# Three open PSUM tiles for the first items of a convolution and spectral-mixing kernel

## The chip, the core and the metric

The kernel runs on one core of a Trainium2 chip. Its time is the device time of one execution in microseconds (us); of several executions the median is given. The engines are TensorE (PE: matmuls; PEld: its weight loads), VectorE (DVE), ScalarE (ACT), GpSimd (POOL) and SyncE (SP). Each takes its own instructions in order, and they meet through semaphores.

## The reference

```python
x = causal_conv(x, softmax(weight))      # 7 taps, one set for each of 8 groups of 24 columns
X = rfft(x, axis=1)[:, :64]              # x: (8, 3264, 192)
Yr = Xr @ w_r[m] - Xi @ w_i[m]           # for each of 64 modes m: two 192 x 192 matrices
Yi = Xr @ w_i[m] + Xi @ w_r[m]
u = x + irfft(Y, n=3264)
out = u + relu(u @ w_ch)                 # (8, 3264, 192) float32
```

## The kernel before

Batches are taken in pairs: `q` (0 to 3) is a pair, and a row tile `t` has 128 rows (t = 0 to 24, and a half tile at the end). The order of the instructions on each engine is the order in which the program writes them; nothing is rescheduled.

Stage 1 loads x, convolves it on TensorE and accumulates the 64 modes. Stage 2 has three kinds of work in one loop over `g` = 0 to 15 (`mix(g)`, L452):

- **Mixing g** multiplies four modes with their two weight matrices: 12 matmuls (L457) into one of two PSUM banks, `low[0]` and `low[1]`. After every second one ScalarE copies the bank out (L466), TensorE transposes the halves into `low[2]` and `low[3]` (L473), and VectorE and ScalarE copy these to `yet` (L480, L482). The weights of g = 8 to 11 are loaded by GpSimd (L446) when mixing g - 8, which had the same buffer, has ended, those of 12 to 15 when mixing g - 4 has. For the last pair of mixings, 14 and 15, these steps are made one by one.
- **Transposes of x**: `c_bank` (L405) makes up to eight 128 x 128 transposes into one bank of a ring of four banks `r`; the helper `copy` brings the bank to `cc`, each third time by ScalarE (L378), else by VectorE (L380).
- **Products ahead**: the output takes `u @ w_ch`, of which the part `x @ w_ch` needs only `cc` and `wc`. For eight of the output's items, and for the half tiles (`c_halves`, L506), it is made in this loop (`c_ahead`, L521: 12 matmuls into two ring banks, two copies of 384 columns) and kept in SBUF. `FREED` (L597) says after which mixing.

`zw_lower(q)` (L561) multiplies the lower 32 modes of pair q with `w_ch` in a ring bank, and copies it to `zw` (L569, L571). It stands after mixings 8 to 11.

Stage 3 makes 53 items (`duos`). An item is two row tiles of a pair of batches, mostly the same t for two pairs: 128 x 768 values in a PSUM tile of two banks. Four such tiles (`za`, `zb`) are used in turn. `c_part(n)` (L531) puts the product with c into the tile with 12 matmuls; an item made ahead has it copied in by ScalarE instead (L717). Then follow `m_part(n, 0)` (L551, the inverse transform times w_ch), Relu in place (`relu`, L613), `m_part(n, 1)` on top (the inverse transform itself), the addition of x by VectorE (`finish`, L638) and the store: by SP for items 0 to 3, which are two neighbouring row tiles (L651, two stores each), by GpSimd for the others (L646). The upper 32 modes of pairs 2 and 3, `(2, 3)`, and the half tiles, `("h",)`, are entries of their own in the list, 25 and 44.

Between the stages stand, in this order: mixing 15, `c_part(0)`, the transposes of mixing 15, the first half of `c_part(1)`, the products of the upper modes of pairs 0 and 1 (L561) in `low[0]` and `low[2]`, their copies, and the second half of `c_part(1)`. Only the tiles of items 0 and 1 are open then; the other two take the place of `low`.

Of the kernel before, what the change touches and what calls it, by code (L numbers as in the profile page):

```python
# [19 lines left out]
def kernel(  # L20
# [32 lines left out]
    def sb(name, shape, dtype, **kw):  # L53
        return pool.tile([P] + shape, dtype, tag=name, name=name, **kw)
# [9 lines left out]
    cc = sb("cc", [NQ, CB, P], BF16, align_bytes=256)  # L64

    MH = MODES // 2
    ftab = sb("ftab", [NT + 1, 2 * MODES], BF16)
    ftab4 = ftab[:, :, :].rearrange("p t (h c m) -> p t h c m", h=2, c=2)

    fupper = sb("fupper", [NT, P], BF16)  # L70
    tabs = (ftab, fupper)

    HD = D // 2
    yet = sb("yet", [2, B, 2, MODES], BF16)


    mixa = sb("mixa", [3 * 2 * B * MODES], BF16)
# [8 lines left out]
    w1 = sb("w1", [3 * HD], BF16)  # L86
    wc = sb("wc", [3, D], BF16)
    ident = sb("ident", [P], BF16)
    perm = sb("perm", [P], BF16)
    ascale = sb("ascale", [1], F32)  # L90
    halfpi = sb("halfpi", [1], F32)
    xs = [sb(f"xs{i}", [2, D], BF16) for i in range(2)]
# [7 lines left out]
        return wts[g] if g < NW + NL else wts[(g - NW - NL) % NW]  # L100


    OB = 2 * 2 * 2 * D
    assert 6 * OB <= NW * WGB and OB == 12 * P

    def place(a):
        return a.bitcast(F32).rearrange("p (k d) -> p k d", k=2)
# [3 lines left out]

    slices = [place(arena[:, OB * i:OB * (i + 1)]) for i in range(6)]
    in_band = place(band[:, :, :].rearrange("p h c -> p (h c)")[:, 0:OB])
    in_cc = [place(cc[:, q, t:t + 12, :].rearrange("p k s -> p (k s)")) for t in (0, 12) for q in range(2)]

    ccf = cc[:, :, :, :].rearrange("p q (t j) s -> p q t (j s)", j=3).bitcast(F32)
# [33 lines left out]

    conv_stack, pp = psum_pool("pconv", "left")
    Z = [pp.tile([P, 2, 512], F32, tag=f"z{i}", name=f"z{i}") for i in range(2)]
    low_stack, pp = psum_pool("plow", "right")
    low = [pp.tile([P, 512], F32, tag=f"low{i}", name=f"low{i}") for i in range(4)]

    def slot(q, t):
        return NT * q + t
# [92 lines left out]
    def load_units(k0, k1):  # L250
        for k in range(k0, k1):
            load_unit(*units[k])
            if k in beside:
# [4 lines left out]
    nc.gpsimd.memset(ident[:], 0.0)  # L258
    nc.gpsimd.affine_select(out=ident[:], in_=ident[:], compare_op=ALU.not_equal, fill=1.0,
                            base=0, pattern=[[-1, P]], channel_multiplier=1)  # L260
    nc.gpsimd.memset(perm[:], 0.0)
    for h in range(2):
        for c in range(2):

# [94 lines left out]
    def xtrans(q, i, bank):  # L359
        tp = low[1 + bank][:, 0:3 * P].rearrange("p (j c) -> p j c", j=3)  # L360
        xsv = xs[q % 2][:, i, :].rearrange("k (p j) -> k j p", j=3)
        for j in range(3):
            nc.tensor.matmul(tp[0:64, j, :], xsv[:, j, :], ident[:], start=True, stop=True,  # L363
                             tile_position=(0, 0), skip_group_check=True)
            nc.tensor.matmul(tp[64:P, j, :], xsv[:, j, :], perm[:], start=True, stop=True,
                             tile_position=(0, 64), skip_group_check=True)
        b = 2 * q + i
        for h in range(2):
            nc.vector.tensor_copy(out=xt[:, h, :, b:2 * B:B, :],
                                  in_=tp[:, :, 64 * h:64 * h + 64].rearrange("p j (c m) -> p j c m", c=2))  # L370
# [78 lines left out]
    for g in range(NL + NW):  # L449
        load_w(g)  # L450

    def mix(g):  # L452
        yp = low[(g // 2) % 2][:, D * (g % 2):D * (g % 2) + D]
        for j in range(3):
            for p4 in range(4):
                m = 4 * g + p4
                nc.tensor.matmul(yp[32 * p4:32 * p4 + 2 * B, :], xt[:, m // MH, j, :, m % MH],  # L457
                                 wbuf(g)[:, p4, j, :], start=(j == 0), stop=(j == 2),
                                 tile_position=(0, 32 * p4), skip_group_check=True)
        if g < NW:  # L460
            load_w(g + NW + NL)
        elif g >= NW + NL:
            load_w(g + NW)

    def mix_copy(d, gs=slice(0, 2)):
        nc.scalar.copy(out=ymix[d % 2][:, gs, :],  # L466
                       in_=low[d % 2][:, 0:2 * D].rearrange("p (g d) -> p g d", g=2)[:, gs, :])

    def mix_trans(d, gs=slice(0, 2)):
        ets = [low[2 + t][:, :].bitcast(BF16)[:, 0:2 * P].rearrange("p (g k) -> p g k", g=2) for t in range(2)]  # L470
        for t in range(2):
            for g in range(gs.start, gs.stop):
                nc.tensor.transpose(ets[t][0:HD, g, :], ymix[d % 2][:, g, HD - HD * t:D - HD * t], ident[:])  # L473
        m = slice(8 * d + 4 * gs.start, 8 * d + 4 * gs.stop)
        for t in range(2):
            dst = yet[0:HD, t, :, :, m].rearrange("p b c m -> p c b m")
            srcv = ets[t][0:HD, gs, :].rearrange("p g (q k) -> p (g q) k", q=4)[:, :, 0:16].rearrange(
                "p m (c b) -> p c b m", c=2)
            if t == 0:
                nc.vector.tensor_copy(out=dst, in_=srcv)  # L480
            else:
                nc.scalar.copy(out=dst, in_=srcv)  # L482
# [71 lines left out]
    def zw_part(q, h, z):  # L554


        for t, w in enumerate((wm, w1)):
            for i in range(2):
                for c in range(2):
                    p0 = 64 * i + 32 * c  # L560
                    nc.tensor.matmul(z[p0:p0 + MH, HD - HD * t:2 * D - HD * t],  # L561
                                     yet[0:HD, t, 2 * q + i, c, MH * h:MH * h + MH], w[0:HD, :],
                                     start=(t == 0), stop=(t == 1), tile_position=(0, p0), skip_group_check=True)

    def zw_copy(q, h, z, act, w=slice(0, 4)):
# [7 lines left out]
    def zw_lower(q):  # L573
        next_bank()
        z = ring[(tbank[0] - 1) % len(ring)]
        zw_part(q, 0, z)
        zw_copy(q, 0, z, q % 2)

    duos = [((q, t), (q, t + 1)) for q in range(2) for t in (0, 2)]
    duos += [((q, t), (q + 1, t)) for q in (0, 2) for t in range(0 if q else 4, NF)]  # L580

    duos[-1:] = [(u,) for u in duos[-1]]
    for k, item in ((25, (2, 3)), (44, ("h",))):
        duos.insert(k, item)

    def is_zw(n):
# [2 lines left out]


    AHEAD = {}
    for (n1, n2), p1 in zip(((8, 13), (18, 23), (30, 35), (40, 48)), [in_band] + slices):
        (q, t1), (_, t2) = duos[n1][0], duos[n2][0]
        AHEAD[n1], AHEAD[n2] = four(p1), ccf[:, q:q + 2, t1:t2 + 1:t2 - t1, :]
        assert duos[n1] == ((q, t1), (q + 1, t1)) and duos[n2] == ((q, t2), (q + 1, t2)) and (q or t1 > 7)

    FREED = {8: (8,), 9: (13,), 12: (18, 23), 13: (30, 40), 14: (35, 48)}  # L597

    free = [in_cc[0], slices[4], slices[5], in_cc[1], slices[3]]
    LATER = {7: (in_band,), 9: (in_cc[2], in_cc[3]), 17: (slices[0],), 29: (slices[1],), 39: (slices[2],)}  # L600
    buffers = []
    for n, duo in enumerate(duos):
        for p in LATER.get(n, ()):
# [11 lines left out]
    def finish(n):  # L615
# [16 lines left out]
        if len(duo) == 1:  # L632
            nc.vector.tensor_tensor(out=ov[:, 0:2, :], in0=zt[:, :, 0:D], in1=xall[:, s[0], :, :], op=ALU.add)
            dst = bass.AP(tensor=out.tensor, offset=out.offset + (2 * q0 * S + P * t0) * D,
                          ap=[[D, P], [S * D, 2], [1, D]])
            (nc.gpsimd if n < N - 1 else nc.sync).dma_start(out=dst, in_=ov[:, 0:2, :])
            return
        nc.vector.tensor_tensor(out=o[:, :, :].rearrange("p k (i d) -> p i k d", i=2),  # L638
                                in0=zt[:, :, 0:2 * D].rearrange("p i (k d) -> p i k d", k=2),
# [13 lines left out]
    N = len(duos)  # L653
    items = [[duo, None] for duo in duos]

    def assign(Z):
        for k, item in enumerate(items):
            if k % 4 in Z:
                item[1] = Z[k % 4]

    PLAN = (2, 2, 3, 2, 3, 2, 2, 2, 3, 3, 3, 3, 99, 99, 99)
    for g in range(NG - 1):
        mix(g)
        if g == NG - 2:
            mix_copy(g // 2, slice(0, 1))
        elif g % 2:
            mix_copy(g // 2)
        some(PLAN[g], NT * (NQ - 1) if g < NW + NL - 1 else NT * NQ)
        for n in FREED.get(g, ()):
            c_ahead(n)  # L670
        if g == NG - 3:
            c_halves()
        if g == NG - 2:
            mix_trans(g // 2, slice(0, 1))
        elif g % 2:
            mix_trans(g // 2)
        if NG // 2 <= g < NG // 2 + NQ:
            zw_lower(g - NG // 2)
    ring_stack.close()
    stack, pp = psum_pool("pz0", "left")  # L680
    ctx.push(stack)
    assign({k: pp.tile([P, 2, 512], F32, tag=f"za{k}", name=f"za{k}") for k in (0, 1)})
    mix(NG - 1)
    mix_copy(NG // 2 - 1, slice(1, 2))
    c_part(0)
    mix_trans(NG // 2 - 1, slice(1, 2))
    c_part(1, (0,))
    for q in range(2):
        zw_part(q, 1, low[2 * q])
    for w in QUARTERS:  # L690
        zw_copy(0, 1, low[0], w == QUARTERS[1], w)
    zw_copy(1, 1, low[2], False)
    c_part(1, (1,))
    low_stack.close()
    stack, pp = psum_pool("pz1", "right")
    ctx.push(stack)
    assign({k: pp.tile([P, 2, 512], F32, tag=f"zb{k}", name=f"zb{k}") for k in (2, 3)})

    def set_up(n):

# [11 lines left out]
    for n in range(N + 1):  # L712
# [5 lines left out]
        elif given(n + 2):  # L718
            nc.scalar.copy(out=items[n + 2][1][:, :, 0:2 * D].rearrange("p k (a d) -> p k a d", a=2),
                           in_=halves.rearrange("p (k a) d -> p k a d", k=2))  # L720

        soon = given(n + 1) or given(n + 2) or given(n + 3) and not given(n - 1)
        if n > 0 and not soon and not given(n):
            set_up(n + 1)
        if 0 < n and not is_zw(n - 1):
            m_part(n - 1, 1)
            finish(n - 1)
        if n > 0 and soon:
            set_up(n + 2 if given(n + 1) else n + 1)


# [28 lines left out]
```

## Time and profile before

Nine runs of the kernel before have a median of 176.71 us (176.59 to 177.59). The profiled execution took 177.59 us, of which its trace covers a span of 174.1 us; 3.5 us lie around it. All times below are us from the start of that span.

| | PE | PEld | DVE | ACT | POOL | DMA |
|---|---|---|---|---|---|---|
| busy in the span | 147.1 (84%) | 108.2 (62%) | 119.4 (69%) | 105.7 (61%) | 100.6 (58%) | mean 231 GB/s |

The mixings start at 74.42, the last of them at 107.14. The first output item is added at 111.62 and its stores are issued from 112.60; the last addition ends at 168.18, and the transfers end in the stretch from 170 to 172. The granted TensorE clock is 1.00 of full speed in every stretch from 30 to 160. In a row of the timeline the columns are start, length, engine, line, operation, output<-input, shape and count, then in brackets the idle time before it and what ended it. A row can stand for several merged instructions; a matmul's length contains its way through the array, so the starts of neighbouring rows say more of TensorE's pace than the lengths do. In a row of the chain the columns are start, length and what ran.

### The profile page before, as it was taken

To read this page: it belongs to the slowest core of one execution; us is meant where nothing else is said; L and a number is where in the kernel's file an instruction comes from. 1 tells how busy PE (TensorE), PEld (TensorE's weight loads), DVE (VectorE), ACT (ScalarE), POOL (GpSimd) and SP (SyncE) were. 2 spreads that over 40 slices of the span, in tenths; PEclk is the share of its full clock that TensorE was granted. 3 is DMA by queue.
4 is the path that set the end of the run, shared out by engine and by line. 5 is a ranking of instruction groups with operands and counts; after the bars stand their busy time and mean duration, and the time that the engine had idled before them with its cause. 6 is when DMAs were issued, how large, how long until landed. Compare 5 with 4: busy or idle time off the path is not lost.

```text
span 174.1 us, 6407 instructions
## 1 busy us (share of the span) xinstructions
PE 147.1 (84%) x2768; PEld 108.2 (62%) x2768; DVE 119.4 (69%) x181; ACT 105.7 (61%) x149; POOL 100.6 (58%) x157
## 2 busy tenths in 40 slices
PE   0056659999999999797999999999999999999930
PEld 0034426666666666576788876887778678875720
DVE  1878653684875677354678785498889879887860
ACT  8166662636444643535566765678888788787820
POOL 7999999867967544353224400006776657666560
PEclk9999997999999999999999999999999999999985
DMA  4999999999999999999999992089898998999994
GB/s 44 164 174 188 190 190 190 193 190 192 190 193 187 200 207 205 207 209 204 207 207 206 206 203 45 4 274 349 339 349 323 362 357 350 361 359 349 314 369 182
DMA packets 44331, 40.17 MB, mean 231 GB/s; under 512 B 28800, under 2 KB 40656, under 8 KB 44304
## 3 DMA queue, kind: packets, MB, share of 16 engines
q0 software_dynamic: 41136, 37.59, 108.8%
q1 hardware_dynamic: 3168, 2.19, 3.9%
q8 instruction: 21, 0.34, 0.8%
q14 instruction: 6, 0.05, 0.1%
HBM read 39.40 MB, written 20.05 MB: 342 GB/s over the span
## 4 chain that ended last, share of the span: by engine, by line
PE 46%; POOL 19%; issue 14%; DVE 7%; DMA 5%; ACT 5%; POOLq 1%; DVEq 0%; ACTq 0%
POOL out_dram L646 17%; PE z L324 13%; PE low L350 9%; DMA arena<-in_moe_w_i_dram 5%; PE r L405 5%; PE low L405 4%; PE low L457 3%; DVE arena L203 2%; PE r L394 2%; PE za L531 2%; PE za L551 2%; PE zb L551 1%; PE low L363 1%; DVE xall L344 1%; POOL xall L165 1%
## 5 line engine op out<-in xcount | busy, mean ns | idle before, releaser
L165 POOL DMA_DIRECT2D xall<-in_x_dram x48 | 38.4, 807 | 5.6 <-DMA xall<-in_x_dram 3.2
L324 PE MATMUL z<-xall,band 64*64 64x192 bf16 (+3 forms) x816 | 27.5, 264 | 16.3 <-ACT band L209 10.5
L344 DVE CAST xall<-z 128x768 bf16<-128x768 f32 (+1 forms) x24 | 24.5, 1021 | 14.7 <-PE z L324 13.5
L646 POOL DMA_DIRECT2D out_dram<-arena x23 | 17.3, 754 | 29.8 <-DVE arena L638 27.3
L342 ACT CAST xall<-z 128x768 bf16<-128x768 f32 (+1 forms) x24 | 20.4, 851 | 22.3 <-PE z L324 21.2
L324 PEld LDWEIGHTS <-band 64*64 64x64 bf16 x816 | 18.3, 110 | 24.9 <-ACT band L209 10.9
L531 PEld LDWEIGHTS <-cc 64*128 64x128 bf16 x504 | 22.7, 94 | 6.2 <-issue 2.8
L613 ACT ACTIVATE za<-za 128x768 f32<-128x768 f32 (+1 forms) x26 | 19.9, 781 | 5.7 <-PE za L551 5.1
L613 ACT ACTIVATE zb<-zb 128x768 f32<-128x768 f32 (+1 forms) x26 | 20.1, 781 | 5.0 <-PE zb L551 4.6
L350 PE MATMUL low<-xall,ftab 128*128 128x384 bf16 x100 | 21.7, 344 | 0.0
L405 PEld LDWEIGHTS <-xall 128*128 128x128 bf16 x300 | 18.7, 105 | 3.3 <-issue 0.3
L380 DVE COPY cc<-r 128x1024 bf16<-128x1024 bf16 (+2 forms) x23 | 14.0, 631 | 6.1 <-PE r L405 2.7
L551 PEld LDWEIGHTS <-ftab 64*128 64x128 bf16 x220 | 14.1, 94 | 5.7 <-issue 1.9
L551 PE MATMUL zb<-mixa,ftab 64*128 64x384 bf16 (+1 forms) x112 | 17.4, 309 | 0.0
L551 PE MATMUL zb<-mixa,fupper 64*128 64x384 bf16 (+1 forms) x112 | 17.4, 308 | 0.0
L551 PE MATMUL za<-mixa,ftab 64*128 64x384 bf16 (+1 forms) x108 | 16.7, 308 | 0.5 <-ACT za L613 0.4
L551 PE MATMUL za<-mixa,fupper 64*128 64x384 bf16 (+1 forms) x108 | 16.7, 308 | 0.0
L446 POOL DMA_DIRECT2D arena<-in_moe_w_r_dram x12 | 7.4, 616 | 15.7 <-PE low L457 10.8
L646 POOL DMA_DIRECT2D out_dram<-cc x17 | 12.8, 754 | 4.6 <-DVE cc L638 2.9
L638 DVE TENSOR_TENSOR arena<-za,xall 128x768 f32<-128x768 f32 x14 | 13.3, 955 | 2.3 <-PE za L551 1.4
L531 PE MATMUL zb<-wc,cc 64*128 64x192 bf16 x258 | 14.5, 243 | 0.0
L531 PE MATMUL za<-wc,cc 64*128 64x192 bf16 x246 | 14.0, 243 | 0.3 <-DVE cc L638 0.2
(126 smaller groups left out, 243.2 us busy)
## 6 DMA issues: line engine op xcount, KB each, us to landing
out_dram<-arena POOLq DMA_DIRECT2D x23, 384.0 KB, 4.7
out_dram<-cc POOLq DMA_DIRECT2D x17, 384.0 KB, 4.7
xall<-in_x_dram POOLq DMA_DIRECT2D x24, 192.0 KB, 7.1
xall<-in_x_dram POOLq DMA_DIRECT2D x16, 240.0 KB, 6.6
arena<-in_moe_w_r_dram POOLq DMA_DIRECT2D x12, 288.0 KB, 9.2
arena<-in_moe_w_i_dram POOLq DMA_DIRECT2D x12, 288.0 KB, 9.3
out_dram<-band POOLq DMA_DIRECT2D x5, 384.0 KB, 4.7
xall<-in_x_dram POOLq DMA_DIRECT2D x8, 144.0 KB, 6.7
```

The source lines that it names most:

```text
L165: nc.gpsimd.dma_start(out=xall[:, s0:s0 + nf, i, :], in_=src)
L324: mm = nc.tensor.matmul(ov[c], band[r, h, c.start + shift + 64 * (r is UP and c is LO): c.start + shift + 64 * (r is UP and c is LO) + 64] ...
L342: nc.scalar.copy(out=dst, in_=srcv)
L344: nc.vector.tensor_copy(out=dst, in_=srcv)
L350: nc.tensor.matmul(xp, ftab[:, t, :], xall[:, slot(q, t), :, :], start=(t == 0), stop=False, skip_group_check=True)
L380: nc.vector.tensor_copy(out=out, in_=in_)
L405: nc.tensor.transpose(tp[:, P * k:P * k + P], src, ident[:])
L531: nc.tensor.matmul(zt[:, i, D * k:D * k + D], cc[r, q, 3 * t + j, :], wc[r, j, :], start=(k == 0 and j == 0), stop=False, skip_group_check ...
L551: nc.tensor.matmul(zt[:, i, D * k:D * (k + w)], tabs[c][r, t, :], zw[r, c, q:q + w, QUARTERS[which], :], start=False, stop=end and k + w = ...
L613: nc.scalar.activation(out=zt[:, :, 0:w], in_=zt[:, :, 0:w], func=ACT.Relu)
L638: nc.vector.tensor_tensor(out=o[:, :, :].rearrange("p k (i d) -> p i k d", i=2), in0=zt[:, :, 0:2 * D].rearrange("p i (k d) -> p i k d", k=2),
L646: nc.gpsimd.dma_start(out=dst, in_=ov)
```

## The change

Item 0 becomes two single items, one row tile each (numbers 0 and 1); there are 54 entries now, and each later one has a number that is one higher. Three PSUM tiles for the items (`z0` to `z2`, six banks) are opened after mixing 14, and `c_part(0)`, `c_part(1)` and `c_part(2)` stand there, ahead of mixing 15. They hold what the items 0 and 1 held before. For this the ring and the banks `low[0]` and `low[1]` are closed at that point, so that mixings 14 and 15 write to `low[2]`, the bank that the transposes of all mixings use too. The products ahead of eight items are spread differently: after mixings 8, 9, 10 and 11 one each, after 12 and 13 two each, none after 14 (before: one after 8 and 9, two after 12, 13 and 14). To have room for the result of the third, `yet`'s lower half, the end of `ftab` and `perm` are put into one piece of SBUF, `early`, that is free once the four `zw_lower` have run; these stand two by two after mixings 8 and 9. The items made ahead are now every fifth; the entries `(2, 3)` and `("h",)` stand at 26 and 34. One more buffer for finished items is free from the start.

```diff
+    ND = NG // 2
+    def mix_bank(d):
+        return low[d % 2] if d < ND - 1 else low[2]
...
-        ets = [low[2 + t][:, :].bitcast(BF16)[:, 0:2 * P].rearrange("p (g k) -> p g k", g=2) for t in range(2)]
+        ets = [low[2 + t][:, c:c + P].bitcast(BF16).rearrange("p (g k) -> p g k", g=2)
+               for t, c in enumerate((2 * D if d == ND - 1 else 0, 0))]
...
+    duos[0:1] = [(u,) for u in duos[0]]
     duos[-1:] = [(u,) for u in duos[-1]]
-    for k, item in ((25, (2, 3)), (44, ("h",))):
+    for k, item in ((26, (2, 3)), (34, ("h",))):
...
-    for (n1, n2), p1 in zip(((8, 13), (18, 23), (30, 35), (40, 48)), [in_band] + slices):
+    for (n1, n2), p1 in zip(((9, 14), (19, 24), (29, 39), (44, 49)), [in_band, in_early] + slices):
...
-    FREED = {8: (8,), 9: (13,), 12: (18, 23), 13: (30, 40), 14: (35, 48)}
+    FREED = {8: (9,), 9: (14,), 10: (19,), 11: (24,), 12: (29, 39), 13: (44, 49)}
...
+        if g in (NG // 2, NG // 2 + 1):
+            for q in range(2):
+                zw_lower(2 * (g - NG // 2) + q)
         for n in FREED.get(g, ()):
             c_ahead(n)
         if g == NG - 3:
             c_halves()
         if g == NG - 2:
+            ring_stack.close()
+            low_stack.close()
+            for k in range(3):
+                open_z(k, "left")
+                c_part(k)
             mix_trans(g // 2, slice(0, 1))
         elif g % 2:
             mix_trans(g // 2)
-        if NG // 2 <= g < NG // 2 + NQ:
-            zw_lower(g - NG // 2)
...
     mix(NG - 1)
-    mix_copy(NG // 2 - 1, slice(1, 2))
-    c_part(0)
-    mix_trans(NG // 2 - 1, slice(1, 2))
-    c_part(1, (0,))
+    mix_copy(ND - 1, slice(1, 2))
+    mix_trans(ND - 1, slice(1, 2))
     for q in range(2):
-        zw_part(q, 1, low[2 * q])
+        zw_part(q, 1, low[2 + q])
...
-    c_part(1, (1,))
...
-            (nc.gpsimd if n < N - 1 else nc.sync).dma_start(out=dst, in_=ov[:, 0:2, :])
+            (nc.sync if n < 2 or n == N - 1 else nc.gpsimd).dma_start(out=dst, in_=ov[:, 0:2, :])
...
+        if n == 1:
+            continue
+        if n == 2:
+            m_part(0, 1)
+            finish(0)
```

`mix_bank(d)` is new: the bank of the pair d of mixings, of ND = 8. `open_z(k, side)`, new too, opens tile k of the four and gives it to every fourth entry from k on.

More of the change, by code (lines that the diff above doesn't have):

```diff
@@ L66 @@
     MH = MODES // 2
-    ftab = sb("ftab", [NT + 1, 2 * MODES], BF16)
+    OB = 2 * 2 * 2 * D
+    YH = 2 * B * 2 * MH
+    early = sb("early", [NT * P + OB], BF16)
+    ftab = early[:, 0:(NT + 1) * P].rearrange("p (t k) -> p t k", t=NT + 1)
+    in_early = early[:, NT * P:NT * P + OB]
+    perm = early[:, (NT + 1) * P + YH:(NT + 2) * P + YH]
+    assert (NT + 2) * P + YH <= NT * P + OB
     ftab4 = ftab[:, :, :].rearrange("p t (h c m) -> p t h c m", h=2, c=2)
@@ L73 @@
     HD = D // 2
-    yet = sb("yet", [2, B, 2, MODES], BF16)
+    yupper = sb("yupper", [2, B, 2, MH], BF16)
+    yet = (early[:, (NT + 1) * P:(NT + 1) * P + YH].rearrange("p (t b c m) -> p t b c m", t=2, b=B, c=2), yupper)
     mixa = sb("mixa", [3 * 2 * B * MODES], BF16)
@@ L88 @@
     ident = sb("ident", [P], BF16)
-    perm = sb("perm", [P], BF16)
     ascale = sb("ascale", [1], F32)
@@ L100, in wbuf @@
         return wts[g] if g < NW + NL else wts[(g - NW - NL) % NW]
-    OB = 2 * 2 * 2 * D
     assert 6 * OB <= NW * WGB and OB == 12 * P
@@ L113 @@
     in_band = place(band[:, :, :].rearrange("p h c -> p (h c)")[:, 0:OB])
+    in_early = place(in_early)
     in_cc = [place(cc[:, q, t:t + 12, :].rearrange("p k s -> p (k s)")) for t in (0, 12) for q in range(2)]
@@ L152 @@
     Z = [pp.tile([P, 2, 512], F32, tag=f"z{i}", name=f"z{i}") for i in range(2)]
+    last_stack, pp = psum_pool("plast", "right")
+    low = [pp.tile([P, 512], F32, tag=f"low{i}", name=f"low{i}") for i in (2, 3)]
     low_stack, pp = psum_pool("plow", "right")
-    low = [pp.tile([P, 512], F32, tag=f"low{i}", name=f"low{i}") for i in range(4)]
+    low[0:0] = [pp.tile([P, 512], F32, tag=f"low{i}", name=f"low{i}") for i in (0, 1)]
     def slot(q, t):
@@ L260 @@
                             base=0, pattern=[[-1, P]], channel_multiplier=1)
-    nc.gpsimd.memset(perm[:], 0.0)
+    nc.gpsimd.memset(perm, 0.0)
     for h in range(2):
@@ L364, in xtrans @@
                              tile_position=(0, 0), skip_group_check=True)
-            nc.tensor.matmul(tp[64:P, j, :], xsv[:, j, :], perm[:], start=True, stop=True,
+            nc.tensor.matmul(tp[64:P, j, :], xsv[:, j, :], perm, start=True, stop=True,
                              tile_position=(0, 64), skip_group_check=True)
@@ L450 @@
         load_w(g)
+    ND = NG // 2
+    def mix_bank(d):
+        return low[d % 2] if d < ND - 1 else low[2]
     def mix(g):
-        yp = low[(g // 2) % 2][:, D * (g % 2):D * (g % 2) + D]
+        yp = mix_bank(g // 2)[:, D * (g % 2):D * (g % 2) + D]
         for j in range(3):
@@ L466, in mix_copy @@
         nc.scalar.copy(out=ymix[d % 2][:, gs, :],
-                       in_=low[d % 2][:, 0:2 * D].rearrange("p (g d) -> p g d", g=2)[:, gs, :])
+                       in_=mix_bank(d)[:, 0:2 * D].rearrange("p (g d) -> p g d", g=2)[:, gs, :])
     def mix_trans(d, gs=slice(0, 2)):
-        ets = [low[2 + t][:, :].bitcast(BF16)[:, 0:2 * P].rearrange("p (g k) -> p g k", g=2) for t in range(2)]
+        ets = [low[2 + t][:, c:c + P].bitcast(BF16).rearrange("p (g k) -> p g k", g=2)
+               for t, c in enumerate((2 * D if d == ND - 1 else 0, 0))]
         for t in range(2):
@@ L473, in mix_trans @@
                 nc.tensor.transpose(ets[t][0:HD, g, :], ymix[d % 2][:, g, HD - HD * t:D - HD * t], ident[:])
-        m = slice(8 * d + 4 * gs.start, 8 * d + 4 * gs.stop)
+        h, m0 = divmod(8 * d, MH)
+        m = slice(m0 + 4 * gs.start, m0 + 4 * gs.stop)
         for t in range(2):
-            dst = yet[0:HD, t, :, :, m].rearrange("p b c m -> p c b m")
+            dst = yet[h][0:HD, t, :, :, m].rearrange("p b c m -> p c b m")
             srcv = ets[t][0:HD, gs, :].rearrange("p g (q k) -> p (g q) k", q=4)[:, :, 0:16].rearrange(
@@ L561, in zw_part @@
                     nc.tensor.matmul(z[p0:p0 + MH, HD - HD * t:2 * D - HD * t],
-                                     yet[0:HD, t, 2 * q + i, c, MH * h:MH * h + MH], w[0:HD, :],
+                                     yet[h][0:HD, t, 2 * q + i, c, :], w[0:HD, :],
                                      start=(t == 0), stop=(t == 1), tile_position=(0, p0), skip_group_check=True)
@@ L595 @@
         assert duos[n1] == ((q, t1), (q + 1, t1)) and duos[n2] == ((q, t2), (q + 1, t2)) and (q or t1 > 7)
-    FREED = {8: (8,), 9: (13,), 12: (18, 23), 13: (30, 40), 14: (35, 48)}
-    free = [in_cc[0], slices[4], slices[5], in_cc[1], slices[3]]
-    LATER = {7: (in_band,), 9: (in_cc[2], in_cc[3]), 17: (slices[0],), 29: (slices[1],), 39: (slices[2],)}
+    FREED = {8: (9,), 9: (14,), 10: (19,), 11: (24,), 12: (29, 39), 13: (44, 49)}
+    free = [in_cc[0], slices[4], slices[5], in_cc[1], slices[3], slices[2]]
+    LATER = {8: (in_band,), 10: (in_cc[2], in_cc[3]), 28: (slices[0],), 43: (slices[1],)}
     buffers = []
@@ L654, with open_z @@
     items = [[duo, None] for duo in duos]
[L656 to L659, printed above, removed]
+    def open_z(k, side):
+        stack, pp = psum_pool(f"pz{k}", side)
+        ctx.push(stack)
+        zt = pp.tile([P, 2, 512], F32, tag=f"z{k}", name=f"z{k}")
+        for item in items[k::4]:
+            item[1] = zt
     PLAN = (2, 2, 3, 2, 3, 2, 2, 2, 3, 3, 3, 3, 99, 99, 99)
@@ L676 @@
             mix_trans(g // 2)
-        if NG // 2 <= g < NG // 2 + NQ:
-            zw_lower(g - NG // 2)
[L679 to L682, printed above, removed]
     mix(NG - 1)
-    mix_copy(NG // 2 - 1, slice(1, 2))
-    c_part(0)
-    mix_trans(NG // 2 - 1, slice(1, 2))
-    c_part(1, (0,))
+    mix_copy(ND - 1, slice(1, 2))
+    mix_trans(ND - 1, slice(1, 2))
     for q in range(2):
-        zw_part(q, 1, low[2 * q])
+        zw_part(q, 1, low[2 + q])
     for w in QUARTERS:
-        zw_copy(0, 1, low[0], w == QUARTERS[1], w)
-    zw_copy(1, 1, low[2], False)
-    c_part(1, (1,))
[L694 to L697, printed above, removed]
+        zw_copy(0, 1, low[2], w == QUARTERS[1], w)
+    zw_copy(1, 1, low[3], False)
+    last_stack.close()
+    open_z(3, "right")
     def set_up(n):
@@ L720 @@
                            in_=halves.rearrange("p (k a) d -> p k a d", k=2))
+        if n == 1:
[3 more added lines that the diff above has]
+            finish(0)
         soon = given(n + 1) or given(n + 2) or given(n + 3) and not given(n - 1)
-        if n > 0 and not soon and not given(n):
+        if n > 1 and not soon and not given(n):
             set_up(n + 1)
@@ L727 @@
             finish(n - 1)
-        if n > 0 and soon:
+        if n > 1 and soon:
             set_up(n + 2 if given(n + 1) else n + 1)
```

## The prediction

> **What bounds the kernel now.** First the busy time by stretch (columns: stretch, its length, busy PE, PEld, DVE, ACT, POOL, clock, DMA share, which can pass 1, GB/s):
>
> ```profile
> 90.00:100.00 10.00, 10.00 (x207) 8.34 (x205) 8.03 (x16) 6.91 (x11) 4.12 (x7) 1.00 1.21 205
> 100.00:110.00 10.00, 9.52 (x206) 6.88 (x205) 7.16 (x16) 5.44 (x13) 0.00 (x0) 1.00 0.64 110
> ...
> 120.00:130.00 10.00, 10.00 (x164) 7.84 (x161) 8.72 (x10) 8.18 (x12) 6.80 (x10) 1.00 0.90 346
> ```
>
> Ahead of the last mixing TensorE and the weight loads are both full; in the output TensorE is full and the stores come close. Then the chain of work that ended last, at the seam:
>
> ```profile
> 97.26 0.60 POOL arena L446
> 97.86 9.23 DMA arena<-in_moe_w_i_dram
> 107.14 0.45 PE low L457 x12
> 107.59 0.60 PE za L531 x12
> 108.78 0.60 PE low L561 x16
> 110.17 0.80 ACT za L613
> ```
>
> Mixing 15 waits for its weights until 107.14. How long TensorE itself has nothing to do there is in the timeline:
>
> ```profile
> 90.31 0.68 PE L521 MATMUL r<-wc,cc 64*128 64x192 bf16 x12
> 90.41 1.01 ACT L378 COPY cc<-r 128x1024 bf16<-128x1024 bf16 x1 [0.88 <-PE r L405]
> ...
> 104.57 0.42 PE L473 MATMUL low<-ident,xs 128*96 128x128 bf16 x4
> ...
> 104.92 0.45 PE L457 MATMUL low<-arena,mixa 128*16 128x192 bf16 x12
> ...
> 105.30 1.25 PE L521 MATMUL r<-wc,cc 64*128 64x192 bf16 x24
> ...
> 105.49 0.28 DVE L480 COPY yet<-low 96x128 bf16<-96x128 bf16 x1
> ...
> 106.47 0.31 PE L473 MATMUL low<-ident,xs 128*96 128x128 bf16 x2
> ...
> 107.14 0.45 PE L457 MATMUL low<-arena,mixa 128*16 128x192 bf16 x12 [0.35 <-DMA arena<-in_moe_w_i_dram]
> ...
> 108.12 0.31 PE L473 MATMUL low<-ident,xs 128*96 128x128 bf16 x2
> ...
> 108.41 0.22 DVE L480 COPY yet<-low 96x64 bf16<-96x64 bf16 x1 [1.08 <-PE low L473]
> ...
> 108.71 0.31 PE L561 MATMUL low<-wm,yet 96*32 96x288 bf16 x4
> ```
>
> Only 0.36 us (106.78 to 107.14) is free ahead of mixing 15. From 88.47, the start of mixing 8, on each row starts where the one before ends, apart from ring waits of 0.1 to 0.3. After 109.58, the first inverse transform, the waits show POOL waiting for VectorE's additions, and these for TensorE or Relu, never for a transfer; full stores land in a median of 4.3 to 5.0 us from the first part of the output to the last. So TensorE sets the pace there too: 5.41 us between the additions of items 10 and 15.
>
> **The change, part by part.** *Ahead of mixing 15.* All eight products ahead stay there and the products of the first three items (24 matmuls) join them: what the two products at 105.30 take, 106.47 - 105.30 = 1.17. Nothing leaves but the wait of 0.36. In the old order those products stood after mixing 15, where they were free: the first tile's ran while ScalarE copied the mixing out (107.52 to 107.96), the second's beside the copies to yet and zw.
>
> *Ring waits.* Ring banks are taken in turn. After mixing 8 there are now two `zw_lower` and then the first product ahead, so it falls on the third and fourth banks; the fourth holds the transposes that ScalarE copies from 90.41 to 91.42, and its matmuls alternate between both. Before, it took the first two and started at 90.31. TensorE would be there at 90.30 + 2 x 0.25 = 90.80 and goes on at about 91.45: 0.6, less the 0.17 that the old order waited: 0.4. After mixing 9 the product follows three banks of transposes and two `zw_lower`; VectorE has two copies of 0.5, one of 0.56 and one of 0.69 in its queue and frees the second bank near 94.95, TensorE comes at 94.5: 0.45, less the 0.16 there now: 0.3. The others meet a ScalarE copy once each (29 and 39): 0.15. Bounds: 0 and 1.3 in all; I take 0.85.
>
> *Mixing 14 in low[2].* It must wait until VectorE has copied the transposes of mixing 13 out. Now that copy ends at 105.77, while mixing 14 starts at 104.92 in another bank. VectorE comes to it late because it has the copies of two products and of the half tiles ahead of it; one of the two half-tile copies falls to ScalarE in the new count. From 0.3 (the copy follows the transposes at once, as at 108.41: 0.29 + 0.28 + 0.08, less 0.36) to 0.9 (as late as now); I take 0.6. Behind it on TensorE stand the new products, so they don't fill it.
>
> *Mixing 15 in the same bank.* It writes columns 192 to 383, the transposes just ahead lie in 384 to 511. By addresses nothing is to wait for, and in the old order mixing 15 waits for its weights alone. The Trainium skill, "PSUM — Partial Sum Buffer", section "PSUM bank collisions raise a hardware error", says that two engines must be kept apart by bank and quadrant and not by address; and the order of the changed kernel's instructions has such a wait on VectorE's copy. By the row at 108.12, copy and restart take until 108.71, 0.59 from the start of the transposes instead of 0.31: 0.28. By addresses the sum would be 0.28 less; I take the rule.
>
> *Weight loads.* Mixing 11 moves back by some 1.6 (0.25 + 0.6 + 0.7), and so does the last load, 97.86 to about 99.5. The DMA share is 1.2 until 104, so it queues either way; even with its own 9.23 in full it lands at 108.7, ahead of the new mixing 15. Nothing.
>
> Sum: 1.17 + 0.85 + 0.6 + 0.28 - 0.36 = 2.54 later, mixing 15 at 109.7.
>
> *From mixing 15 to the transform.* The transposes no longer stand behind 12 matmuls: 107.52 + 0.12 + 0.32 + 0.07 = 108.03 instead of 108.12: -0.09. The `zw` copies stay.
>
> *The first items.* In the old order 109.58 to the first store at 112.60 is 3.0. Now item 0 has 4 matmuls (0.16), way through the array and signal 0.26, a Relu of half the size (0.47 by the row at 166.40), 4 matmuls 0.16, 0.25, an addition of 0.55 (167.16): 1.85, so 1.2 sooner. But the tiles hold what two tiles held; the products of the next items (L531) follow the transform as before. Adding 0.16, 0.33 and 0.49 in their new order, the second half of item 2 ends 2.9 after the transform starts, that of old item 1 3.0 after. TensorE gains 0.1 for all that follows, and the early store only 0.4 MB of early transfers, while the stores later wait for TensorE. Two half Relus for one cost ScalarE 0.47 x 2 - 0.80 = 0.14, two half additions VectorE 0.55 x 2 - 0.96 = 0.14; they lie in the gaps of engines busy 8.2 and 8.7 of 10, and cost 0.14 without these. SP issues 2 + 6 stores where it issued 8.
>
> *Same work elsewhere.* Nine entries are given, 43 others are full or half, before as after; every fifth instead of nearly so. The half tiles' four stores (SP, 2.68 us at 160.98) move to the middle, with nothing behind them on SP. The sixth buffer frees nobody: no addition waits for a transfer. Bounds together -0.3 and +0.3; I take 0.
>
> In all 2.54 - 0.09 - 0.1 = 2.35. The profiled execution has 177.59 = 174.1 + 3.5; it would take 179.9. The median lies 0.9 under it: 176.71 + 2.35 = 179.06, say 179.0.
>
> A rule speaks against this: the Trainium skill ("Trainium Kernel Development and Optimization", best practices) judges TensorE's headroom by weight-load time, not by busy matmuls. From 88.4 to 104.9 PEld is busy 13.3 of 16.5 us; the 3.2 left would swallow the 1.17. But those 3.2 are not gaps: the 24 matmuls at 105.30 start 49 ns apart, and nothing starts in between. With the rule, the sum is 1.2; with the starts, 2.35.
>
> **The rivals.** (1) *Evictions keep up.* VectorE is busy 8.0 and ScalarE 6.9 of 10 there, so other waits may vanish as new ones come; no ring wait and mixing 14 late by 0.3: 1.17 + 0.3 + 0.28 - 0.36 - 0.2 = 1.2, 177.9. (2) *Weights late.* The loads queue behind fewer others and land as slowly as the first ones to cc did (11.4 instead of 9.3), at 110.9 for an issue at 99.5: 1.2 more, 180.2. (3) *Faster: the stores bound the output.* Place: the 5 us from 107 to 112 without any transfer. If the DMA share of 0.90 is all that it can give, the end follows the first store, which comes 1.2 sooner after the transform. It decides as soon as mixing 15 slips by less than 1.2, that is, if the products fill gaps that I took for work: 176.71 - 1.2 = 175.5 with no slip. For it: the transfers' tail of 4 us after the last addition. Against: stretches of 2 us with 0.98 beside others of 0.79, and POOL waiting for additions. (4) *It does nothing*: slip and early store cancel: 176.7.
>
> **How the numbers follow.** Main case 0.60 (178.3 to 179.8), rival 1 0.20 (177.2 to 178.3), rival 2 0.08, rival 3 0.08, rival 4 0.04. The range 177.2 to 180.1 leaves out the last two and half of rival 2, with some of the edges. A measurement of this kernel tells about 0.2% (0.35 us) from no change. Faster 0.08, same 0.04, slower 0.88.
>
> **What would show it.** Right: mixing 15 released by VectorE's copy and not by its weights, near 109.7; a gap of about 0.6 ahead of mixing 14; a gap of 0.6 in the product after mixing 8; first store 1.85 after the first transform; POOL still waiting for additions; an end that lies as far behind the transform as now, less 0.2. Wrong: mixing 15 by 107.5, or additions that wait for transfers.

## The result and the profile after

The changed kernel has a median of 178.97 us (178.27 to 180.20, 16 runs); 53 runs of the kernel before have one of 176.99 us. The ratio is 1.0112 (95%: 1.0092 to 1.0131): 1.98 us slower, between 1.6 and 2.3. Predicted were 179.0 us and a difference of 2.35. The profiled execution took 179.2 us with a span of 177.0.

The busy time by stretch of the changed kernel, in the columns of before:

```profile
90.00:100.00 10.00, 9.69 (x190) 7.28 (x178) 7.41 (x14) 6.34 (x11) 3.66 (x6) 1.00 1.21 206
100.00:110.00 10.00, 8.95 (x181) 7.05 (x179) 5.91 (x13) 4.90 (x12) 0.00 (x0) 1.00 0.64 109
...
120.00:130.00 10.00, 10.00 (x168) 8.06 (x169) 8.60 (x10) 8.18 (x12) 6.84 (x10) 1.00 0.92 349
```

TensorE, full between 90 and 100 before, has lost 0.31 there, and another 0.57 between 100 and 110, at the same clock and the same DMA share. The stretch from 120 to 130, in the output, is as before. The chain of work that ended last, at the seam:

```profile
104.83 0.57 DVE arena L391
...
105.44 1.15 PE r L525 x24
...
106.87 0.30 DVE yupper L499
...
107.21 0.45 PE low L474 x12
107.65 1.09 PE z L550 x24
108.75 0.26 PE low L491 x2
...
109.04 0.23 DVE yupper L499
...
109.32 0.47 PE low L474 x12
...
111.30 0.37 DVE mixa L590
...
111.69 0.34 ACT mixa L588
...
112.07 0.48 ACT z L633
...
112.59 0.34 PE z L570 x4
```

The load that stood in this chain is gone. In its place come the 24 new matmuls (107.65) and two copies by VectorE, of which one holds up mixing 14 (107.21) and one mixing 15 (109.32). The timeline shows how long TensorE waits for each:

```profile
90.23 0.24 PE L540 MATMUL r<-wc,cc 64*128 64x192 bf16 x1
...
90.78 0.65 PE L540 MATMUL r<-wc,cc 64*128 64x192 bf16 x11 [0.31 <-ACT cc L389]
...
107.21 0.45 PE L474 MATMUL low<-arena,mixa 128*16 128x192 bf16 x12 [0.27 <-DVE yupper L499]
...
109.32 0.45 PE L474 MATMUL low<-arena,mixa 128*16 128x192 bf16 x12 [0.33 <-DVE yupper L499]
```

The first two rows are the product after mixing 8: its first matmul runs, its second waits for ScalarE's copy of the bank beside it. From starts to starts, with the steps of before in brackets, the mixings 8 to 15 take 3.58 (2.72), 3.76 (3.27), 2.43 (2.06), 2.79 (2.29), 3.34 (3.14), 3.53 (2.97), 2.11 (2.22): 21.54 us (18.67), 2.87 more.

That is more than the medians differ by, and two more executions of the kernel before (the last experiment below) say why. All in us from the start of the span:

| execution | mixing 8 | mixing 15 | 8 to 15 | first transform | last addition ends |
|---|---|---|---|---|---|
| before, first profile | 88.47 | 107.14 | 18.67 | 109.58 | 168.18 |
| before, second | 87.61 | 107.62 | 20.01 | 110.06 | 168.66 |
| before, third | 88.21 | 107.24 | 19.03 | 109.68 | 168.29 |
| changed | 87.78 | 109.32 | 21.54 | 111.42 | 170.13 |
| changed, two stores held back | 88.26 | 109.81 | 21.55 | 111.92 | 170.70 |

In the old order mixing 15 comes when its weights come (107.14 to 107.62), though mixing 8 starts up to 0.86 apart; in the new one TensorE's own row of work sets it, and takes 21.54 and 21.55 us. Against the mean of the three (19.24) the mixings lose 2.30, the way from mixing 15 to the transform gains 0.34 (2.10 instead of 2.44), and the output loses 0.11 (58.71 instead of 58.60 to the last addition): 2.07, within the interval of 1.6 to 2.3. A mean of three executions is a rough one; the median of 53 runs is what the 1.98 rests on.

### The profile page after: what moved, and what is told of

It reads as the page before. It is cut to its first block, busy times and chain, and to the rows that moved or that the text cites. A ratio compares the mean times of both kernels' runs of the same rounds, so it can differ in the third digit from the quotient of the medians.

```text
span 177.0 us, 6418 instructions
## 1 busy us (share of the span) xinstructions
PE 148.8 (84%) x2768; PEld 108.8 (61%) x2768; DVE 119.5 (67%) x182; ACT 105.7 (60%) x150; POOL 100.6 (57%) x157
## 3 DMA queue, kind: packets, MB, share of 16 engines
q1 hardware_dynamic: 3168, 2.19, 3.9%
## 4 chain that ended last, share of the span: by engine, by line
PE 58%; POOL 22%; issue 6%; DMA 4%; ACT 4%; DVE 2%; POOLq 1%; DVEq 0%; ACTq 0%
POOL xall L176 14%; PE z L570 13%; PE z L550 9%; PE z L335 7%; PE r L416 7%; PE low L361 6%; POOL out_dram L666 5%; DMA xall<-in_x_dram 4%; PE low L474 4%; PE r L540 3%; PE low L416 2%; PE r L405 2%; PE low L491 2%; ACT z L633 1%; POOL xall L247 1%
## 5 line engine op out<-in xcount | busy, mean ns | idle before, releaser
L633 ACT ACTIVATE z<-z 128x768 f32<-128x768 f32 (+1 forms) x53 | 39.8, 770 | 10.4 <-PE z L570 9.5
L570 PE MATMUL z<-mixa,early 64*128 64x384 bf16 (+1 forms) x220 | 33.8, 309 | 0.7 <-ACT z L633 0.4
L570 PE MATMUL z<-mixa,fupper 64*128 64x384 bf16 (+1 forms) x220 | 33.7, 308 | 0.0
L550 PE MATMUL z<-wc,cc 64*128 64x192 bf16 x504 | 28.2, 243 | 0.0
L658 DVE TENSOR_TENSOR arena<-z,xall 128x768 f32<-128x768 f32 x24 | 22.7, 956 | 5.5 <-PE z L570 3.0
L361 PE MATMUL low<-xall,early 128*128 128x384 bf16 x100 | 22.0, 348 | 0.0
L658 DVE TENSOR_TENSOR cc<-z,xall 128x768 f32<-128x768 f32 x19 | 18.0, 954 | 1.0 <-ACT z L633 0.4
L570 PEld LDWEIGHTS <-early 64*128 64x128 bf16 x220 | 14.4, 94 | 6.5 <-issue 2.6
L389 ACT COPY cc<-r 128x1024 bf16<-128x1024 bf16 (+1 forms) x13 | 11.0, 848 | 7.8 <-PE r L416 4.1
L570 PEld LDWEIGHTS <-fupper 64*128 64x128 bf16 x220 | 12.1, 94 | 1.2 <-issue 0.2
```

The costliest lines, as they stand in the source:

```text
L361: nc.tensor.matmul(xp, ftab[:, t, :], xall[:, slot(q, t), :, :], start=(t == 0), stop=False, skip_group_check=True)
L550: nc.tensor.matmul(zt[:, i, D * k:D * k + D], cc[r, q, 3 * t + j, :], wc[r, j, :], start=(k == 0 and j == 0), stop=False, skip_group_check ...
L570: nc.tensor.matmul(zt[:, i, D * k:D * (k + w)], tabs[c][r, t, :], zw[r, c, q:q + w, QUARTERS[which], :], start=False, stop=end and k + w = ...
L633: nc.scalar.activation(out=zt[:, :, 0:w], in_=zt[:, :, 0:w], func=ACT.Relu)
```

## The experiments

Each ratio is to the kernel before, with its 95% interval; 0.001 of it is 0.18 us. "Changed" stands for the kernel after the change.

**The products ahead of zw_lower.** This undoes the ring wait after mixing 8 and leaves all else.

```diff
+        for n in FREED.get(g, ()):
+            c_ahead(n)
         if g in (NG // 2, NG // 2 + 1):
             for q in range(2):
                 zw_lower(2 * (g - NG // 2) + q)
-        for n in FREED.get(g, ()):
-            c_ahead(n)
```

> The changed kernel with one edit: after mixings 8 and 9 the product ahead stands before the two zw_lower and not behind them. My theory (ring waits cost 0.7 us of the loss): the waits of 0.5 after mixing 8 and about 0.4 after mixing 9 shrink, since the product finds the first two ring banks free; a second zw_lower still meets ScalarE's copy after mixing 8 (0.3). So 0.3 to 0.7 us faster than the changed kernel, about 1.008 of before. Rival (evictions keep up in sum, the wait only moves): the same as the changed kernel, 1.011.

Measured: 1.0106 (1.0074 to 1.0137). The step after mixing 8 is 3.25 instead of 3.58, the one after mixing 9 stays (3.74): the wait only moved from `zw_lower` to the product. The trace has 0.34 less, the medians show between nothing and 0.4: inconclusive, the interval is wider than the effect.

**The three products behind mixing 15.** Their tiles stay open early.

```diff
                 open_z(k, "left")
-                c_part(k)
...
     mix_copy(ND - 1, slice(1, 2))
+    c_part(0)
     mix_trans(ND - 1, slice(1, 2))
+    c_part(1)
...
     zw_copy(1, 1, low[3], False)
+    c_part(2)
```

> The changed kernel with the products of items 0, 1 and 2 put back behind mixing 15 (one beside ScalarE's copy, one beside the copies to yet, the third beside those to zw); the three tiles stay open as early. My theory (24 matmuls of 1.17 us stood on the path of mixing 15): mixing 15 comes 1.17 earlier after mixing 14, and the products cost at most 0.2 where they stand now: 0.9 to 1.2 us faster than the changed kernel, about 1.005 of before. Rival (the loss lies in the ring and in low[2] alone, the products filled gaps): no faster than the changed kernel, or slower by what they take behind mixing 15.

Measured: 1.0102 (1.0058 to 1.0147), some 0.2 better than the changed kernel by the ratio and 0.5 by the medians. My theory had 0.9 to 1.2, and the times alone are too wide to exclude 0.9; the trace makes it a miss: from the start of mixing 8 to the end of the last addition this kernel takes 82.04 us and the changed one 82.35, only 0.3 less. The timeline of this kernel shows where the rest is:

```profile
106.83 0.45 PE L474 MATMUL low<-arena,mixa 128*16 128x192 bf16 x12 [0.27 <-DVE yupper L499]
...
107.69 0.31 PE L491 MATMUL low<-ident,xs 128*96 128x128 bf16 x2 [0.42 <-ACT xs L483]
...
108.33 0.45 PE L474 MATMUL low<-arena,mixa 128*16 128x192 bf16 x12 [0.32 <-DVE yupper L499]
```

From mixing 14 to 15 it takes 1.50 instead of 2.11, so only 0.6 of 1.17 is saved: with nothing between, TensorE waits 0.42 for ScalarE to copy mixing 14 out, time that the products had filled (they had covered it). And 0.3 comes back later: the transform on top of the first Relu starts 3.56 after mixing 15 instead of 3.27.

**The shared bank alone.** In the kernel before, mixings 14 and 15 go to `low[2]`.

```diff
+    def mix_bank(d):
+        return low[d % 2] if d < NG // 2 - 1 else low[2]
```

> The kernel before with one edit: mixings 14 and 15 write to low[2], where the transposes lie. My theory: mixing 14 waits for VectorE's copy of the transposes of 13, which ends 0.85 after it would start, and mixing 15 for the copy ahead of it (0.28), less the 0.36 that mixing 15 waits for its weights now: 0.7 to 0.9 us slower than before, 1.004 to 1.005. Rival (the products behind mixing 14 would have had to wait for their ring copies anyway): within 0.3 us of before.

Measured: 1.0049 (1.0031 to 1.0067), 0.9 us, as my theory had it. Its timeline has the same two waits, here without a new product anywhere:

```profile
105.97 0.45 PE L460 MATMUL low<-arena,mixa 128*16 128x192 bf16 x12 [0.83 <-DVE yet L484]
...
108.35 0.44 PE L460 MATMUL low<-arena,mixa 128*16 128x192 bf16 x12 [0.60 <-DVE yet L484]
```

**The first two stores held.** In the changed kernel, the stores of items 0 and 1 are issued behind those of item 2.

```diff
+            if n < 2:
+                held.append((dst, ov[:, 0:2, :]))
...
+            while held:
+                dst, src = held.pop(0)
+                nc.sync.dma_start(out=dst, in_=src)
```

> The changed kernel with the stores of items 0 and 1 held back until those of item 2 are issued, some 2.2 us later than now; nothing else changes. My theory (TensorE sets the pace of the output, the early stores are worth nothing): the same as the changed kernel within 0.2 us, 1.011 of before. Rival (the transfers bound the output and its end follows its first store): 1 to 2 us slower than the changed kernel.

Measured: 1.0118 (1.0079 to 1.0157), as the changed kernel, with the first store at 116.37 instead of 113.61. By the intervals the early stores are worth less than 0.9 us, and in the traces, from mixing 8 to the last addition, 0.1 (82.44 instead of 82.35). My rival, 1 to 2 us, is out.

**A bank of their own.** In the changed kernel, mixings 14 and 15 keep `low[1]`; so only two tiles can be open, and 12 matmuls are ahead instead of 24.

```diff
-        return low[d % 2] if d < ND - 1 else low[2]
+        return low[d % 2]
...
-            low_stack.close()
-            for k in range(3):
+            for k in range(2):
                 open_z(k, "left")
...
     zw_copy(1, 1, low[3], False)
+    c_part(2)
```

> The changed kernel, but mixings 14 and 15 keep a bank of their own (low[1]), so only two tiles are opened early: the products of items 0 and 1 stand ahead of mixing 15 as in the changed kernel, those of item 2 (12 matmuls) beside the copies to zw. My theory: mixing 14 follows the transposes at once (0.3 sooner), mixing 15 no longer waits for VectorE (0.3), and 12 matmuls leave its path (0.5, since ScalarE's copy then shows), of which up to 0.3 come back behind it: 0.8 to 1.1 us faster than the changed kernel, about 1.006 of before. Rival (the shared bank is hidden behind other waits): at most 0.3 us faster.

Measured: 1.0057 (1.0035 to 1.0079), by the ratios 1.0 us faster than the changed kernel. Mixings 14 and 15 have no wait in its timeline:

```profile
107.25 0.45 PE L474 MATMUL low<-arena,mixa 128*16 128x192 bf16 x12
...
108.23 0.31 PE L490 MATMUL low<-ident,xs 128*96 128x128 bf16 x2
...
108.48 0.45 PE L474 MATMUL low<-arena,mixa 128*16 128x192 bf16 x12
```

**Singles and spread alone.** The last kernel, with `c_part(0)` and `c_part(1)` behind mixing 15 too, and the products ahead of `zw_lower`.

```diff
     mix_copy(ND - 1, slice(1, 2))
+    c_part(0)
     mix_trans(ND - 1, slice(1, 2))
+    c_part(1)
```

> Of the changed kernel only the new places of the products ahead and the two single first items are left: own bank for mixings 14 and 15, the products of items 0 to 2 behind mixing 15, the products ahead before the zw_lower. Behind mixing 14 TensorE then has nothing but transposes, and waits for ScalarE's copy. My theory: 1.0 to 1.3 us faster than the changed kernel, but 0.6 to 0.9 slower than before (ring waits, and the two products that used to stand behind mixing 14 now stand ahead of it, where nothing was free): about 1.004. Rival (the spread costs nothing once the bank and the early products are undone): 1.000 of before.

Measured: 1.0030 (1.0013 to 1.0047), 0.5 us slower than before and 1.5 faster than the changed kernel: a little better than my theory (0.6 to 0.9 and 1.0 to 1.3), and apart from the rival's 1.000.

**Singles alone.** Own bank, no product of the first items ahead, `zw_lower` one by one, and the eight items made ahead where the kernel before made them (in numbers of the new list):

```diff
-    FREED = {8: (9,), 9: (14,), 10: (19,), 11: (24,), 12: (29, 39), 13: (44, 49)}
+    FREED = {8: (9,), 9: (14,), 12: (19, 24), 13: (29, 44), 14: (39, 49)}
```

> Of the change only the two single first items, the items made ahead at every fifth place and the half tiles' earlier place are left; products ahead stand after mixings 8, 9, 12, 13 and 14 and zw_lower one by one as before, mixings 14 and 15 have a bank of their own, the first three items' products stand behind mixing 15. My theory (an early store brings nothing, TensorE gains 0.1 to 0.2): 0 to 0.3 us faster than before. Rival (the transfers bound the output): 1.0 to 1.2 us faster than before, 0.994.

Measured: 1.0005 (0.9979 to 1.0030). Early first items gain nothing even where nothing is paid for them: were the stores what bounds the output, this kernel would be at 0.994. Its mixings stand in the old order, and wait for weights at mixing 11 and at mixing 15:

```profile
96.67 0.45 PE L474 MATMUL low<-arena,mixa 128*16 128x192 bf16 x12 [1.13 <-DMA arena<-in_moe_w_i_dram]
...
107.86 0.45 PE L474 MATMUL low<-arena,mixa 128*16 128x192 bf16 x12 [0.56 <-DMA arena<-in_moe_w_i_dram]
```

From mixing 8 to 15 it takes 20.65 us, so 19.24 is not a fixed length of the old order.

**The new spread with cover.** As the one before, but with the changed kernel's spread and paired `zw_lower`; only the last two products stay behind mixing 14 instead of 13.

```diff
-    FREED = {8: (9,), 9: (14,), 10: (19,), 11: (24,), 12: (29, 39), 13: (44, 49)}
+    FREED = {8: (9,), 9: (14,), 10: (19,), 11: (24,), 12: (29, 39), 14: (44, 49)}
```

> As b2_singles_only, but four products ahead stand after mixings 8 to 11 and the zw_lower two by two as in the changed kernel; two products stand behind mixing 14 as before, none after 13. As much work stands ahead of mixing 15 as before. My theory: only the ring waits remain of the loss, 0.7 to 1.0 ahead of mixing 15, less 0.36 of the wait for weights and 0.2 for the singles: 0.2 to 0.5 us slower than before, 1.001 to 1.003. Rival (evictions keep up): equal to b2_singles_only.

Measured: 1.0001 (0.9978 to 1.0023), equal to before within 0.4 us. My theory, that the ring waits of the spread cost 0.2 to 0.5, doesn't show in the time (its lower half is not excluded), though the waits are there: mixing 13 comes 15.89 after mixing 8, as in the changed kernel (15.90), where before had 13.48. Its timeline at the end:

```profile
105.67 0.45 PE L474 MATMUL low<-arena,mixa 128*16 128x192 bf16 x12
106.05 1.25 PE L539 MATMUL r<-wc,cc 64*128 64x192 bf16 x24
...
107.23 0.31 PE L490 MATMUL low<-ident,xs 128*96 128x128 bf16 x2
...
107.66 0.45 PE L474 MATMUL low<-arena,mixa 128*16 128x192 bf16 x12
```

Mixing 15 starts at 107.66 with no wait for its weights; the second execution of before started it at 107.62 after one. From mixing 8 to 15 it takes 19.42 us, where the three executions of before have a mean of 19.24. What the spread loses is, but for 0.2, time that the old order spends on waiting for weights.

**The products twice.** In the changed kernel, the 24 matmuls ahead of mixing 15 are made a second time into the same tiles.

```diff
             for k in range(3):
                 open_z(k, "left")
                 c_part(k)
+            for k in range(3):
+                c_part(k)
```

> The changed kernel with the products of items 0, 1 and 2 made twice ahead of mixing 15 (24 matmuls more, the second set replaces the first). My theory (TensorE is the path to mixing 15 there and has no gap left): 1.1 to 1.2 us slower than the changed kernel, 1.018 of before. Rival (mixing 15 has slack behind its weights or a copy): less than 0.5 us slower.

Measured: 1.0181 (1.0126 to 1.0235), by the ratios 1.2 us over the changed kernel, which the two intervals fix only to between 0.2 and 2.2. The trace is narrower: mixing 15 follows mixing 14 after 3.09 instead of 2.11, 0.98 more. No gap is left that would take them.

**The kernel before again**, twice, unchanged.

> The kernel before, for a second trace. The runs so far (s1_spread_covered and b2_singles_only as fast as before, although their mixing 15 comes at 107.7 and 107.9 and not at 107.14) suggest that in most executions of the kernel before mixing 15 waits longer for its weights than the 0.36 us of the first trace. If so, it starts here at 107.4 to 107.9 after a wait of 0.5 to 1.0; if not, near 107.1 after 0.3 to 0.4.

> The kernel before once more, for a third trace, with the same two readings as r1_before_again.

Measured: 1.0001 (0.9983 to 1.0019) for the first; 176.85 us in one run for the second. The waits view of the first one (us in all, how many, longest):

```profile
PE low L457 <- DMA arena<-in_moe_w_i_dram: 1.6, 4, 0.6
```

Its timeline, and then that of the second, at mixing 15:

```profile
107.62 0.45 PE L457 MATMUL low<-arena,mixa 128*16 128x192 bf16 x12 [0.55 <-DMA arena<-in_moe_w_i_dram]
```

```profile
107.24 0.45 PE L457 MATMUL low<-arena,mixa 128*16 128x192 bf16 x12 [0.71 <-DMA arena<-in_moe_w_i_dram]
```

The first starts mixing 15 where the runs had suggested, the second near the old place but after a longer wait. So the same program waits 0.36, 0.71 or 1.6 us for the weights of the mixings from 8 on; of the 1.6, 0.45 lie ahead of mixing 8 and 1.15 between it and mixing 15 (0.19, 0.41 and 0.55).

Put in a row, the kernels make a ladder, each one further step of the change: spread and singles with cover 1.0001; the two products taken from behind mixing 14: 1.0030, 0.5 us; 12 matmuls of the first items in their place: 1.0057, 0.5 us; 12 more, and the shared bank: 1.0112, 1.0 us. By the intervals each step is known to about 0.5 us, so the first two are barely apart from nothing by the times alone; the traces, from the start of mixing 8 to the end of the last addition, rise in the same order: 80.50, 81.14, 81.53 and 82.35 us. (The second also has its products ahead of `zw_lower`, which by the first experiment is worth 0.4 at the most.)

## Why the prediction was right, step by step

The mechanism is the one forecast: TensorE ahead of mixing 15 is full, and what is put there is paid for, less the wait for weights. That the median came so near (178.97 for 179.0) is luck: the nine runs that the forecast started from lie 0.28 under the median of the 53, and its difference of 2.35 lies 0.37 above the measured one. By its own terms:

- *The 24 matmuls, 1.17.* Right: doubled, they cost 1.2 by the ratios and 0.98 in the trace. The Trainium skill ("Trainium Kernel Development and Optimization", section "Best Practices") judges the distance to the roofline (the best that the chip could do) by two measures, the share of the peak matmul rate and the share of weight-load time. The prediction took the second alone, by which 3.2 us were left, and did not follow it; the kernel with the products twice bears that out, there was no room. (Where it calls the weight loads full, its rows have them at 8.34 and 6.88 of 10.) But taking the 24 away brings only 0.2 to 0.5, as they cover ScalarE's copy of mixing 14 (0.42). The old order had that cover from the two products behind mixing 14; the change moved those ahead, to mixing 13, and put the 24 in their place. The prediction saw only load in what stands ahead of mixing 15, and no cover.
- *The wait of 0.36 that disappears.* Undersized: between mixing 8 and 15 it is 0.36 in the one execution that I had, and 0.71 and 1.15 (of the 1.6) in two others. With the mean of the three traces, mixing 15 slips by 2.30 from mixing 8 and not 2.87. This term, not the sum of the costs, is why 2.35 was too much: without its wait of 0.35 the first execution takes 18.32, so the costs are 21.54 - 18.32 = 3.22 where the prediction had 2.90, and the waits, with what they hold up, take 19.24 - 18.32 = 0.92 where it had 0.36.
- *Ring waits, 0.85.* By the traces more: the five steps from mixing 8 to 13 add 0.86, 0.49, 0.37, 0.50 and 0.20 = 2.42, less 1.2 for the two products of 0.6 that now stand ahead of mixing 13, so 1.2. The place is right (after mixing 8, for ScalarE's copy: 0.55 from the first matmul of the product to its second, where 0.6 was forecast). Alone, without the other steps of the change, they cost less than 0.4 us, since the weights are waited for anyway.
- *Mixing 14 in low[2], 0.6.* Too high by itself: it starts 0.69 after the transposes instead of 0.35, so 0.34, near the lower bound of 0.3. VectorE wasn't late, its copy began at once (106.87). The other 0.2 of that step (3.53 instead of 2.97) is the half tiles' wait for VectorE's copy of the products' bank (105.44).
- *Mixing 15 behind the copy, 0.28.* Measured 0.33, and with both waits taken away and 12 matmuls less, 1.0 us come back; put into the kernel before, the shared bank costs 0.9. The columns are disjoint, and the program waits all the same, as the rule of the Trainium skill ("PSUM — Partial Sum Buffer", section "PSUM bank collisions raise a hardware error") asks: apart by bank and quadrant and not by address. No run leaves the wait out, so what the chip would do without it is not shown.
- *Weight loads, nothing.* Right: the last was issued at 98.91 and had landed at 107.1, more than 2 us ahead of mixing 15; the rival "weights late" is out.
- *From mixing 15 to the transform, -0.09.* By the first matmul it was -0.34, as six matmuls of the second product (109.32 to 109.58 before) no longer stand ahead of it: 0.26 that the prediction left out. But TensorE stands still for about as long right behind:

```profile
111.42 0.26 PE L570 MATMUL z<-mixa,early 64*128 64x192 bf16 x2
...
111.71 0.26 PE L570 MATMUL z<-mixa,fupper 64*128 64x192 bf16 x2
```

The first two matmuls need only the lower modes; the next two need the upper ones, and start when VectorE's copy of these ends (111.30 to 111.67 in the chain). Before, they followed at once (109.74). That copy starts 1.98 after mixing 15 instead of 2.05, 0.07 sooner, close to the 0.09. Where the products used to run beside ScalarE's copy of mixing 15, TensorE now waits 0.42 for it (at 110.18).

- *The first items, 1.2 sooner, worth 0.1.* The first store comes 2.19 after the transform instead of 3.02, so 0.8 sooner; the last addition doesn't: 58.71 us after the transform instead of 58.60. The sum had the first Relu 0.42 after the transform's start and it comes after 0.65, behind the wait just shown and ScalarE's half of a `zw` copy (111.69 in the chain). Counted from mixing 15 this and the term above fit as one: the first store is 1.17 sooner (4.29 instead of 5.46) where 0.09 + 1.2 was forecast, the end 0.23 sooner (60.81 instead of 61.04) where 0.09 + 0.1 was.
- *The stores as the bound* (the rival on the other side) is excluded by two kernels: with the stores held back the loss of 1 to 2 us that it asks for does not come, and single items without the price don't gain its 1.0.

What stays open is how much of the ring waits is still paid in the changed kernel: without the 0.34 after mixing 8 the time is the same within 0.4%. Nor was the shared bank tried apart from the last 12 matmuls in the changed kernel. Why mixing 15 gets its weights up to half a microsecond apart in executions of one program is not known.

## What to carry to other kernels

A wait for a transfer on the bounding engine is a budget, and one profile gives one draw of it; profile the unchanged kernel two or three times before a forecast takes such a wait at its length. Work put between a producer and its consumer on the same engine is not only load, it is cover: before it is moved away, ask what copy it hides. And a program that lets matmuls write to a PSUM bank of which another engine empties a different part, with a wait between the two as here, turns two independent steps into a chain; a tile more was not worth that.

## What the runs showed that was not expected

- Mixings 8 to 15 took 18.67, 20.01 and 19.03 us in three executions of one program that waits for loads there, and 21.54 and 21.55 in the changed kernel and its variant with stores held, which don't.
- For the hand-over of a bank from VectorE's copy to a matmul, TensorE idled 0.32 to 0.33 us each time it came ahead of mixing 15 (the changed kernel, the products late, the products twice), whatever stood in front; in the kernel before with the shared bank alone it was 0.83 ahead of mixing 14 and 0.60 ahead of 15, as VectorE had other copies to end first.
